# The first batch of a packed-attention and SoLU kernel: Z and the attention weights as two 16-bit parts instead of pairs of 32-bit words

## The chip, the cores and the metric

The kernel runs on one core of a Trainium2 chip. The metric is the time of one execution on the device, in microseconds (us); lower is better. A kernel is timed in several executions, and their median is compared. One more execution is recorded by the profiler; all durations below come from that one.

## What is computed

Eight batches with 8 heads, 576 query and key rows and 64 columns per head, and 32 packed queries `p` per head. Two attentions follow each other, and a layer of 512 to 1024 to 512 columns works on their output:

```python
def sm_attn(qq, kk, vv):
    s = scale * np.matmul(qq, kk.transpose(0, 1, 3, 2))
    s = s - np.max(s, axis=-1, keepdims=True)
    a = np.exp(s)
    a = a / (np.sum(a, axis=-1, keepdims=True) + 1e-09)
    return np.matmul(a, vv)
p_packed = sm_attn(p, k, v)
out = sm_attn(q, p_packed, p_packed)
...
h = x @ w_in
e = np.exp(h - np.max(h, axis=-1, keepdims=True))
sm = e / (np.sum(e, axis=-1, keepdims=True) + 1e-09)
solu = h * sm
...
ln = (solu - mu) / np.sqrt(var + 1e-06) * g_ln
return (ln @ w_out).astype(np.float32)
```

Here `x` is `out` with the heads side by side: 4608 tokens of 512 columns. The weights `w_in` and `w_out` arrive as 64-bit numbers.

## The kernel before

**The work.** For each batch the packed attention gives 32 rows per head (`pack`, flows k0 to k7), transposed in the tile `ppT`. The second attention never forms its output: `make_z` (flows z0 to z7) multiplies the packed rows by `w_in`, so that a batch has a matrix Z of 256 rows and 1024 columns, and `unpack` (q0 to q7) makes the attention weights `a` of 576 query rows on those 256 rows. A token tile of 128 rows (`token_tile`, t0 to t35) is then h = a Z, followed by softmax, product, normalisation, a transpose by DMA, and the product with `w_out`. As 576 is four and a half times 128, every fifth token tile (t4, t13, t22, t31) takes its upper 64 rows from an even batch and its lower 64 from the odd batch behind it; it is called a shared tile below. A shared tile issues 24 matmuls with 64 columns of weights, where a plain tile issues 12 with 128.

**Precision.** A product of 32-bit quality is made from two parts: high times high, high times low, low times high (lines 636 and 637). For batches 1 to 7 the parts are 16-bit (F16): `zh`, `zl`, `a_h`, `a_l`. Z is scaled by a power of two that is found on the chip: `pack` sums the squares of the packed rows and takes half the exponent (`size`, lines 459 to 465), `weight_size` (flow N) does so for `w_in` (`weight`), and `z_scale` (line 341) puts them together. For batch 0 the parts are 32-bit words of a type that TensorE rounds (F32R): `z_r` and `a_r`, without a scale (`plain`, line 100, is 1). That has three consequences. `pack(0)` returns before the squares (line 455). N isn't needed before batch 1. And the first shared tile, t4, is written differently from the others (lines 625 and 640): all of its matmuls of one batch, then those of the other, while the other shared tiles alternate between the two batches from one matmul to the next:

```python
for x, r, t in ((x, r, t) for x in range(2) for r in range(2) for t in range(3)) if not c else ((x, r, t) for r in range(2) for t in range(3) for x in range(2)):
```

**How Z is split.** `split` (line 578) has two ways for the later batches: 'a' copies the product from PSUM with the scale (ACT), casts the copy and subtracts; 'l' casts from PSUM with the scale (ACT, line 606) and subtracts from PSUM (DVE, line 608). Batch 0 goes by lines 587 to 594: copy by ACT (589), cast by ACT (591), subtract by DVE or POOL (593). `ZF_BY` chooses. Its weights are cast by ACT (line 529) and subtracted by DVE (531).

**The order of the work.** Everything stands in the string `ORDER`: each name there advances that flow (a generator) to its next `yield`. Each engine carries out its own instructions strictly in that order; semaphores do the rest. Names that begin with l are loads (`lw` w_in, `lo` w_out, `lk`, `lq`, `lv`, `lp`, `lg`); W and O convert the weights to 32 bits, S and C scale `w_out`, H splits `w_in` into 16-bit halves that batches 2 to 7 use, Z is a warm-up of TensorE. PSUM has three tiles `h` of two banks, one `po`, one `pa`. `LOAD_IN` says in which buffers a raw weight waits: 'h' and 'l' are the buffers of `zh` and `zl`, 'r' is one of `raw`. The halves of H lie in the buffers of `a_r` (line 332), so H waits until t4 has used them.

Of the kernel before, what the change touches and what calls it, by code (L numbers as in the profile page):

```python
# [47 lines left out]
def packed_attention_solu_kernel(ctx: ExitStack, tc: tile.TileContext, q: bass.AP, k: bass.AP, v: bass.AP, p: bass.AP, w_in: bass.AP, w_out: bass.AP, g_ln: bass.AP, out: bass.AP):  # L48
# [719 lines left out]
```

## Time and profile before

| | us |
|---|---|
| median of 3 executions | 396.0 |
| lowest, highest | 393.84, 396.99 |
| the profiled execution | 393.78 |
| its span, from the first to the last instruction | 392.0 |

The profiled execution is 1.8 us longer than its span, and 2.2 us under the median. Engines are PE (TensorE's matmuls), PEld (its weight loads, beside the matmuls), DVE (VectorE), ACT (ScalarE), POOL (GpSimd) and SP (which issues the DMAs). Matmuls are pipelined: the duration of one (0.38 us) is longer than the distance from one start to the next. A float32 matmul can show as two records. L641 is line 641 of the kernel.

### The profile page before, as it was taken

To read this page: it belongs to the slowest core of one execution; us is meant where nothing else is said; L and a number is where in the kernel's file an instruction comes from. 1 tells how busy PE (TensorE), PEld (TensorE's weight loads), DVE (VectorE), ACT (ScalarE), POOL (GpSimd) and SP (SyncE) were. 2 spreads that over 40 slices of the span, in tenths; PEclk is the share of its full clock that TensorE was granted. 3 is DMA by queue.
4 is the path that set the end of the run, shared out by engine and by line. 5 is a ranking of instruction groups with operands and counts; after the bars stand their busy time and mean duration, and the time that the engine had idled before them with its cause. 6 is when DMAs were issued, how large, how long until landed. Compare 5 with 4: busy or idle time off the path is not lost.

```text
span 392.0 us, 8802 instructions
## 1 busy us (share of the span) xinstructions
PE 379.0 (97%) x3370; PEld 198.5 (51%) x3370; DVE 303.8 (78%) x484; ACT 251.0 (64%) x424; POOL 254.3 (65%) x442
## 2 busy tenths in 40 slices
PE   8798989989999999999999999999999999999996
PEld 8566666445444544554445445544454444444445
DVE  2758889998997977898879689995888868468541
ACT  2468788586786868585556956755667476546630
POOL 2476599984566886587373855884458768764630
PEclk9969999999999999999999999999999999999999
DMA  8999896879897796999798977936643533334661
GB/s 285 420 363 352 194 208 120 194 147 177 192 187 139 184 214 123 166 174 209 162 171 176 171 143 209 219 83 139 137 89 82 134 80 84 110 80 107 108 161 54
DMA packets 213866, 66.11 MB, mean 169 GB/s; under 512 B 194744, under 2 KB 207808, under 8 KB 213312
## 3 DMA queue, kind: packets, MB, share of 16 engines
q1 hardware_dynamic: 213824, 65.56, 72.7%
q8 instruction: 26, 0.43, 0.5%
q14 instruction: 16, 0.13, 0.1%
HBM read 37.23 MB, written 9.44 MB: 119 GB/s over the span
## 4 chain that ended last, share of the span: by engine, by line
PE 89%; DVE 5%; ACT 4%; issue 1%; POOL 0%; DVEq 0%; POOLq 0%
PE po L698 41%; PE h L641 23%; PE h L698 5%; PE h L366 3%; PE pa L444 3%; PE h L396 2%; PE h L569 2%; PE h L515 2%; PE po L117 2%; PE h L434 2%; PE h L203 1%; PE po L119 1%; DVE s L480 1%; ACT e L223 1%; DVE nm L644 1%
## 5 line engine op out<-in xcount | busy, mean ns | idle before, releaser
L698 PE MATMUL po<-wch,yT 128*128 128x512 f16 x512 | 160.1, 379 | 1.2 <-ACT o_sb L704 1.2
L698 PEld LDWEIGHTS <-yT 128*128 128x128 f16 x888 | 85.5, 98 | 103.2 <-issue 5.9
L698 PE MATMUL po<-wcl,yT 128*128 128x512 f16 x256 | 97.0, 379 | 0.0
L672 ACT ACTIVATE yhl<-u,negmu 128x1024 f16<-128x1024 f32 x36 | 41.2, 1145 | 24.6 <-POOL negmu L669 24.4
L666 DVE SCALAR_TENSOR_TENSOR u<-e,s_row,h 128x1024 f32<-128x1024 f32 x36 | 45.8, 1271 | 14.5 <-POOL s_row L658 7.7
L674 DVE SCALAR_TENSOR_TENSOR yhl<-u,negmu,yhl 128x1024 f16<-128x1024 f32 x36 | 48.1, 1335 | 6.1 <-ACT yhl L672 5.7
L644 DVE TENSOR_REDUCE nm<-h 128x1 f32<-128x1024 f32 x36 | 43.7, 1213 | 5.5 <-PE h L641 5.3
L641 PE MATMUL h<-zl,a_h 128*128 128x512 f16 (+1 forms) x160 | 47.8, 380 | 0.0
L680 ACT ACTIVATE e<-u,negmu 128x1024 f32<-128x1024 f32 x36 | 41.0, 1139 | 0.0
L662 ACT ACTIVATE e<-h,nmc,z_scale 128x1024 f32<-128x1024 f32 x32 | 38.4, 1198 | 3.7 <-DVE nmc L647 3.0
L641 PEld LDWEIGHTS <-a_h 128*128 128x128 f16 (+1 forms) x280 | 25.1, 101 | 28.1 <-issue 1.4
L649 ACT ACTIVATE nmc<-nm,z_scale 128x1 f32<-128x1 f32 x29 | 8.5, 292 | 45.4 <-DVE nm L644 45.4
L652 POOL TENSOR_SCALAR bound<-nm,z_scale 128x1 f32<-128x1 f32 x31 | 15.5, 500 | 32.1 <-DVE nm L644 30.2
L641 PE MATMUL h<-zh,a_h 128*128 128x512 f16 (+1 forms) x120 | 35.8, 380 | 0.0
L706 DVE TENSOR_SCALAR o_sb<-po,c_row,inv 128x512 f32<-128x512 f32 x24 | 19.3, 806 | 16.1 <-PE po L698 13.6
L641 PE MATMUL h<-zl,a_l 128*128 128x512 f16 (+1 forms) x80 | 30.3, 379 | 0.0
L688 POOL TENSOR_TENSOR c_row<-c_row,neg_half 128x1 f32<-128x1 f32 x36 | 24.5, 681 | 3.0
L669 POOL TENSOR_SCALAR negmu<-su 128x1 f32<-128x1 f32 x36 | 8.8, 244 | 23.2 <-DVE u L666 20.2
L641 PE MATMUL h<-zh,a_l 128*128 128x512 f16 (+1 forms) x60 | 22.7, 379 | 0.0
L486 POOL TENSOR_TENSOR s<-s,mx 128x576 f32<-128x576 f32 x14 | 17.1, 1228 | 8.2 <-DVE mx L484 8.2
L499 POOL TENSOR_TENSOR a<-a,sm 128x576 f32<-128x576 f32 x16 | 19.7, 1238 | 3.7 <-DVE sm L497 3.1
L531 POOL TENSOR_TENSOR a_l<-s,a_h 128x576 f16<-128x576 f32 x14 | 18.4, 1320 | 4.6 <-ACT a_h L529 4.6
(184 smaller groups left out, 727.7 us busy)
## 6 DMA issues: line engine op xcount, KB each, us to landing
out_dram<-o_sb SPq DMA_DIRECT2D x35, 256.0 KB, 2.3
v_sb<-in_v_dram SPq DMA_DIRECT2D x8, 1024.0 KB, 6.7
raw<-in_k_dram SPq DMA_DIRECT2D x24, 288.0 KB, 4.7
raw<-in_q_dram SPq DMA_DIRECT2D x96, 72.0 KB, 2.5
zl<-in_moe_w_in_dram SPq DMA_DIRECT2D x2, 1024.0 KB, 7.3
raw<-in_k_dram SPq DMA_DIRECT2D x2, 1024.0 KB, 12.1
raw<-in_moe_w_out_dram SPq DMA_DIRECT2D x2, 1024.0 KB, 9.3
zh<-in_moe_w_in_dram SPq DMA_DIRECT2D x2, 1024.0 KB, 13.9
```

The costliest lines, as they stand in the source:

```text
L499: EN(nc, SOFT_BY[2 * b + 1]).tensor_tensor(out=w2, in0=w2, in1=sm.unsqueeze(2).broadcast_to([P, NB, J]), op=ALU.mult)
L531: EN(nc, A2L_BY[2 * b + r]).tensor_tensor(out=lo, in0=a2T, in1=hi if b else hi.bitcast(F32), op=ALU.subtract)
L641: nc.tensor.matmul(dst_[:, cols], lhsT=lhsT, rhs=z[:, r, cols], start=bool(first), stop=bool(last))
L644: nc.vector.tensor_reduce(out=nm, in_=h, axis=AX.X, op=ALU.max, negate=True)
L662: nc.scalar.activation(e, h, AF.Exp, bias=nmc, scale=sc[:, 1:], accum_out=se)
L666: nc.vector.scalar_tensor_tensor(out=u, in0=e, scalar=s_row, in1=h, op0=ALU.mult, op1=ALU.mult, accum_out=su)
L672: nc.scalar.activation(yhl[:, 0], u, AF.Identity, bias=negmu)
L674: nc.vector.scalar_tensor_tensor(out=yhl[:, 1], in0=u, scalar=negmu, in1=yhl[:, 0], op0=ALU.add, op1=ALU.subtract)
L680: nc.scalar.activation(e, u, AF.Square, bias=negmu, accum_out=sq)
L688: nc.gpsimd.tensor_tensor(out=c_row, in0=c_row, in1=neg_half, op=ALU.pow)
L698: nc.tensor.matmul(po[:, cols], lhsT=yT[:, a, c], rhs=w[:, c, cols], start=c == 0 and t == 0, stop=c == NFC - 1 and t == 2)
L706: nc.vector.tensor_scalar(out=o_sb[:, cols], in0=po[:, cols], scalar1=c_row, scalar2=inv, op0=ALU.mult, op1=ALU.mult)
```

## The change

Batch 0 is treated as batches 1 to 7 are. Its special cases go, its scale is made on the chip, t4 is written as the other shared tiles are, H gets buffers of its own, `ZF_BY` sets batch 0 to 'l', one weight load moves from a `zh` to a `zl` buffer, and `ORDER` is another string. The cut diff:

```diff
-ZF_BY = 'aaaallllaaaaaaaaaaaaaaaaaaaaaaaa'
+ZF_BY = 'llllllllaaaaaaaaaaaaaaaaaaaaaaaa'
...
-LOAD_IN = 'hlhlrhrh'
+LOAD_IN = 'hlhlrhrl'
...
-ORDER = 'lw1 lp W1 W1 lk0 W1 Z W1 lo0 lw3 O0 lw2 k0 k0 lp O0 O0 W3
+ORDER = 'lw2 Z W2 lk0 W2 lo0 lp O0 W2 k0 O0 p p k0 lw3 k0 O0 W2 lw1
...
-    a_r = [par.tile([P, 2, S], F32R, name='a_r', bufs=2) for i in range(2)]
...
-        hi = [par.tile([P, 4 * S], F16, name='a_r', bufs=2)[:, :2 * DF].rearrange('p (g f) -> p g f', g=2) for _ in range(2)]
+        hi = [par.tile([P, 2 * DF], F16, name='w_hi', bufs=2).rearrange('p (g f) -> p g f', g=2) for _ in range(2)]
...
-        if not b:
-            return
         squares = att.tile([P, 2 * D], F32, name='squares')
...
-            hi, lo = (a_h[b % 2][:, r], a_l[b % 2][:, r]) if b else (a_r[0][:, r], a_r[1][:, r])
+            hi, lo = (a_h[b % 2][:, r], a_l[b % 2][:, r])
...
-                elif not b:
-                    full = whole[0][:, r, cols]
-                    nc.scalar.copy(full, pz)
-                    yield
-                    copy_by(nc, ZH_BY[at])(z_r[0][:, r, cols], full)
-                    yield
-                    EN(nc, ZL_BY[at]).tensor_tensor(out=z_r[1][:, r, cols], in0=full, in1=z_r[0].bitcast(F32)[:, r, cols], op=ALU.subtract)
-                    yield
...
-            for x, r, t in ((x, r, t) for x in range(2) for r in range(2) for t in range(3)) if not c else ((x, r, t) for r in range(2) for t in range(3) for x in range(2)):
+            for r, t, x in ((r, t, x) for r in range(2) for t in range(3) for x in range(2)):
                 left = slice(0, LEFT) if x else slice(MAIN, S)
-                a_hi, a_lo, z_hi, z_lo = (a_h[x], a_l[x], zh[c + x], zl[c + x]) if c + x else (a_r[0], a_r[1], z_r[0], z_r[1])
+                a_hi, a_lo, z_hi, z_lo = (a_h[x], a_l[x], zh[c + x], zl[c + x])
...
-            for dst_, lhsT, z, r, first, last in terms[6:] + terms[:6] if b is None and not c and n else terms:
+            for dst_, lhsT, z, r, first, last in terms:
                 nc.tensor.matmul(dst_[:, cols], lhsT=lhsT, rhs=z[:, r, cols], start=bool(first), stop=bool(last))
```

**Three places in the order of the instructions.** On PE, where batch 0's second attention and its Z begin (`ppT` is batch 0's; L506 are the scores, L575 the products of Z, L271 a column sum for a scale), before:

```order
L450 MATMUL pa<-ident,pp 128x128
L180 MATMUL po<-ident,g_raw 128x8
L506 MATMUL h<-qT,ppT 32x288 x4
L203 MATMUL h<-ident,e 64x128 x8
L506 MATMUL h<-qT,ppT 32x288 x12
L575 MATMUL h<-w_in_sb,ppT 32x512 x8
L271 MATMUL pa<-ssq,ones_f 128x8
```

The same place now (L500 are the scores, L564 the products, L455 the sum of batch 0's squares, L267 a column sum):

```order
L446 MATMUL pa<-ident,pp 128x128
L368 MATMUL h<-ident,raw 128x128 x2
L199 MATMUL h<-ident,e 64x128 x8
L455 MATMUL pa<-total,ones_f 128x1
L500 MATMUL h<-qT,ppT 32x288 x4
L176 MATMUL po<-ident,g_raw 128x8
L267 MATMUL pa<-wsq,ones_f 128x4
L500 MATMUL h<-qT,ppT 32x288 x8
L564 MATMUL h<-w_in_sb,ppT 32x512 x4
L500 MATMUL h<-qT,ppT 32x288 x4
L564 MATMUL h<-w_in_sb,ppT 32x512 x4
```

The two sums that batch 0's scale needs, of the squares and of `wsq` (the size of `w_in`), have moved between and ahead of the first scores; the sum of `wsq` stood far behind, after t3.

On DVE, the same stretch, from the copy that makes `ppT` on (`s_443` and `s_444` are the scores of the even and the odd heads), before:

```order
L453 COPY ppT<-pa 128x128
L244 TENSOR_REDUCE ssq<-raw 128x2
L480 STREAM_TRANSPOSE s_443<-h 128x288
L225 TENSOR_SCALAR yT<-e 128x1024
L480 STREAM_TRANSPOSE s_443<-h 128x288
L480 STREAM_TRANSPOSE s_444<-h 128x288
L244 TENSOR_REDUCE ssq<-zh 128x2
```

And now:

```order
L449 COPY ppT<-pa 128x128
L240 TENSOR_REDUCE ssq<-raw 128x2
L310 TENSOR_SCALAR size<-pa 128x1
L311 TENSOR_SCALAR size<-size 128x1
L245 TENSOR_SCALAR wsq<-wsq 128x4
L246 TENSOR_SCALAR wsq<-wsq 128x4
L316 SCALAR_TENSOR_TENSOR wsq<-wsq 128x4
L474 STREAM_TRANSPOSE s_452<-h 128x288
L269 TENSOR_REDUCE w_size<-pa 128x1
L310 TENSOR_SCALAR w_size<-w_size 128x1
L311 TENSOR_SCALAR w_size<-w_size 128x1
L319 TENSOR_SCALAR w_size<-w_size 128x1
```

Nine small instructions (two for `size`, three for `wsq`, four for `w_size`) now stand around the first transpose of scores, and two more, for `z_scale`, follow behind them.

On PE, the first shared tile, t4 (batch 0 has the first number of `zh` and `zl`, batch 1 the second), before:

```order
L641 MATMUL h_1180<-zh_495,a_r_117 64x512
L641 MATMUL h_1180<-zl_496,a_r_117 64x512
L641 MATMUL h_1180<-zh_495,a_r_118 64x512
L641 LDWEIGHTS a_h1_120
L641 MATMUL h_1180<-zl_1003,a_h1_120 64x512
```

And now:

```order
L617 LDWEIGHTS a_h0_114
L617 MATMUL h_1225<-zh_498,a_h0_114 64x512
L617 LDWEIGHTS a_h1_115
L617 MATMUL h_1225<-zl_1022,a_h1_115 64x512
L617 LDWEIGHTS a_h0_114
L617 MATMUL h_1225<-zh_498,a_h0_114 64x512
L617 LDWEIGHTS a_h1_115
L617 MATMUL h_1225<-zl_1022,a_h1_115 64x512
```

Batch 0's matmuls stood together, ahead of batch 1's; now they alternate from the first on. Ahead of t4 the order before has 54 of the matmuls with `w_out` (L698), the new one has 72 (L674).

## Rows read from the trace of the kernel before

**Rows 1.** The page, part 1: busy us, share of the span, instructions, by engine.

```profile
PE 379.0 (97%) x3370; PEld 198.5 (51%) x3370; DVE 303.8 (78%) x484; ACT 251.0 (64%) x424; POOL 254.3 (65%) x442
```

**Rows 2.** Windows: stretch, length, busy us (instructions) by engine, granted clock, DMA share, GB/s.

```profile
20.00:30.00 10.00, 9.66 (x92) 6.88 (x94) 5.58 (x8) 5.75 (x10) 7.57 (x4) 0.66 1.10 357
30.00:54.00 24.00, 20.80 (x379) 14.38 (x376) 20.53 (x38) 20.45 (x33) 15.76 (x10) 1.00 0.99 270
54.00:95.00 41.00, 38.95 (x329) 21.64 (x329) 37.74 (x70) 30.49 (x55) 33.77 (x52) 1.00 0.81 155
95.00:389.00 294.00, 293.81 (x2431) 141.31 (x2430) 230.09 (x361) 186.90 (x321) 189.33 (x359) 1.00 0.68 145
```

**Rows 3.** Waits of PE: who waited for whom, us in total, times, longest.

```profile
PE h L396 <- ACT pT L209: 3.5, 1, 3.5
...
PE po L698 <- ACT o_sb L704: 1.2, 1, 1.2
...
PE pa L271 <- DVE ssq L280: 0.7, 1, 0.7
```

**Rows 4.** Timeline of PE: start, us, engine, line, operation, tiles, count.

```profile
55.11 0.62 PE L641 MATMUL h<-zh,a_r 128*128 128x512 f32 x2
55.57 0.39 PE L641 MATMUL h<-zl,a_r 128*128 128x512 f32 x1
55.80 0.61 PE L641 MATMUL h<-zh,a_r 128*128 128x512 f32 x2
...
66.70 0.38 PE L461 MATMUL pa<-total,ones_f 128*128 128x1 f32 x2
66.94 0.48 PE L641 MATMUL h<-zh,a_r 128*128 128x512 f32 x1
```

**Rows 5.** The chain that ended last: start, us, what; w_out's 24 matmuls, three shared tiles.

```profile
161.55 5.18 PE po L698 x24
...
89.48 5.70 PE h L641 x24
...
178.49 2.78 PE h L641 x24
...
261.02 2.71 PE h L641 x24
```

**Rows 6.** Windows of DVE alone: stretch, length, busy us (instructions), clock, DMA share, GB/s.

```profile
35.45:56.30 20.85, 18.33 (x35) 1.00 1.02 229
...
80.00:120.00 40.00, 36.81 (x63) 1.00 0.85 171
```

**Rows 7.** Timeline of DVE: batch 0's subtractions, then the small instructions of batch 1's scale.

```profile
42.87 2.28 DVE L593 TENSOR_TENSOR zl<-zf,zh 128x512 fp32r<-128x512 f32 x2
...
49.84 1.36 DVE L531 TENSOR_TENSOR a_r<-s,a_r 128x576 fp32r<-128x576 f32 x1 [0.42 <-ACT a_r L529]
...
53.84 0.88 DVE L531 TENSOR_TENSOR a_r<-s,a_r 128x576 fp32r<-128x576 f32 x1 [0.64 <-ACT a_r L529]
54.64 1.65 DVE L593 TENSOR_TENSOR zl<-zf,zh 128x512 fp32r<-128x512 f32 x1
...
68.93 0.15 DVE L315 TENSOR_SCALAR size<-size 128x1 int32<-128x1 int32 x1
...
69.42 1.09 DVE L320 SCALAR_TENSOR_TENSOR wsq<-wsq 128x4 f32<-128x4 f32 x1
...
72.90 0.41 DVE L344 TENSOR_TENSOR z_scale<-w_size,size 128x1 int32<-128x1 int32 x1
...
183.79 0.75 DVE L486 TENSOR_TENSOR s<-s,mx 128x576 f32<-128x576 f32 x1
```

**Rows 8.** Batch 1's subtraction of Z: count, ns min/median/max, first and last start, forms.

```profile
L608 DVE SCALAR_TENSOR_TENSOR zl<-h,z_scale,zl x4: 654/710/751, 83.5 to 92.3; 128x512 f16<-128x512 f32 x4
```

**Rows 9.** Timeline of PE: the same kind of matmul within, and behind, the slow stretch.

```profile
21.47 1.84 PE L203 MATMUL h<-ident,e 128*64 128x128 f32 x16
23.24 2.16 PE L396 MATMUL h<-kT,pT 64*32 64x288 f32 x16
25.34 3.48 PE L366 MATMUL h<-ident,raw 128*64 128x128 f32 x32
...
29.77 1.09 PE L203 MATMUL h<-ident,e 128*64 128x128 f32 x16
...
31.16 1.97 PE L366 MATMUL h<-ident,raw 128*64 128x128 f32 x32
```

More of the change, by code (lines that the diff above doesn't have):

```diff
@@ L99, in packed_attention_solu_kernel @@
     nc.gpsimd.memset(neg_one, -1.0)
-    plain = const.tile([P, 2], F32, name='plain')
-    nc.gpsimd.memset(plain[:, :1], 1.0)
-    nc.gpsimd.memset(plain[:, 1:], 1.0 / A_MAX)
     e1 = const.tile([P, 2, S + LEFT], F32, name='e1')
@@ L527, in unpack @@
             yield
-            hi, lo = (a_h[b % 2][:, r], a_l[b % 2][:, r]) if b else (a_r[0][:, r], a_r[1][:, r])
+            hi, lo = (a_h[b % 2][:, r], a_l[b % 2][:, r])
             nc.scalar.copy(hi, a2T)
             yield
-            EN(nc, A2L_BY[2 * b + r]).tensor_tensor(out=lo, in0=a2T, in1=hi if b else hi.bitcast(F32), op=ALU.subtract)
+            EN(nc, A2L_BY[2 * b + r]).tensor_tensor(out=lo, in0=a2T, in1=hi, op=ALU.subtract)
             yield
@@ L535, in make_z @@
         ppT = packed[b]
-        if b:
-            z_scale(b)
-            s_z = zsc[b][:, :1]
-            if b % 2:
-                sc = zsc[b - 1, b] = small.tile([P, 2], F32, name='z_scale2')
-                for x in range(2):
-                    nc.gpsimd.tensor_copy(sc[LEFT * x:LEFT * x + LEFT], zsc.get(b - 1 + x, plain)[LEFT * x:LEFT * x + LEFT])
-            yield
-            parts = par.tile([P, 2, 2, DF], F16, name='zl' if b % 2 else 'zh', bufs=2)
-            zh[b], zl[b] = (parts[:, 0], parts[:, 1])
-            if ZP_BY[b] == '1':
-                s_z = 1.0 / A_MAX
-                s_p = small.tile([P, 1], F32, name='s_p')
-                nc.vector.tensor_scalar(out=s_p.bitcast(I32), in0=size[b].bitcast(I32), scalar1=-1, scalar2=188 << 23, op0=ALU.mult, op1=ALU.add)
-                pph = att.tile([P, 2, P], F16, name='pph')
-                nc.scalar.activation(pph[:, 0], ppT, AF.Copy, scale=s_p)
-                yield
-                nc.vector.scalar_tensor_tensor(out=pph[:, 1], in0=ppT, scalar=s_p, in1=pph[:, 0], op0=ALU.mult, op1=ALU.subtract)
-                yield
-        else:
-            z_r.extend(par.tile([P, 2 * DF], F32R, name=name, bufs=2).rearrange('p (r f) -> p r f', r=2) for name in ('zh', 'zl'))
-            if ZF_BY[0] == 'a':
-                whole[0] = par.tile([P, 2, DF], F32, name='zf')
+        z_scale(b)
+        s_z = zsc[b][:, :1]
+        if b % 2:
+            sc = zsc[b - 1, b] = small.tile([P, 2], F32, name='z_scale2')
+            for x in range(2):
+                nc.gpsimd.tensor_copy(sc[LEFT * x:LEFT * x + LEFT], zsc[b - 1 + x][LEFT * x:LEFT * x + LEFT])
+        yield
+        parts = par.tile([P, 2, 2, DF], F16, name='zl' if b % 2 else 'zh', bufs=2)
+        zh[b], zl[b] = (parts[:, 0], parts[:, 1])
+        if ZP_BY[b] == '1':
+            s_z = 1.0 / A_MAX
+            s_p = small.tile([P, 1], F32, name='s_p')
+            nc.vector.tensor_scalar(out=s_p.bitcast(I32), in0=size[b].bitcast(I32), scalar1=-1, scalar2=188 << 23, op0=ALU.mult, op1=ALU.add)
+            pph = att.tile([P, 2, P], F16, name='pph')
+            nc.scalar.activation(pph[:, 0], ppT, AF.Copy, scale=s_p)
+            yield
+            nc.vector.scalar_tensor_tensor(out=pph[:, 1], in0=ppT, scalar=s_p, in1=pph[:, 0], op0=ALU.mult, op1=ALU.subtract)
+            yield
         banks = [[], []]
@@ L581, in split @@
                 at = 4 * b + 2 * n + r
-                if not b and ZF_BY[0] == 'l':
-                    nc.scalar.copy(z_r[0][:, r, cols], pz)
-                    yield
-                    nc.vector.tensor_tensor(out=z_r[1][:, r, cols], in0=pz, in1=z_r[0].bitcast(F32)[:, r, cols], op=ALU.subtract)
-                    yield
-                elif not b:
-                    full = whole[0][:, r, cols]
-                    nc.scalar.copy(full, pz)
-                    yield
-                    copy_by(nc, ZH_BY[at])(z_r[0][:, r, cols], full)
-                    yield
-                    EN(nc, ZL_BY[at]).tensor_tensor(out=z_r[1][:, r, cols], in0=full, in1=z_r[0].bitcast(F32)[:, r, cols], op=ALU.subtract)
-                    yield
-                elif ZF_BY[at] == 'a':
+                if ZF_BY[at] == 'a':
                     if b not in whole:
```

8 lines of the change are left out of this document (4 added, 4 removed).

## The prediction

> **What bounds the kernel now.** I read the shares of the engines first. PE is busy for 379.0 of 392.0 us, DVE 304, ACT and POOL some 250 [rows 1]. The table by stretches says where the other 13 us lie: from 95 to 389 us PE is busy for 293.81 of 294 us, from 54 to 95 for 38.95 of 41, and only before 54 does it miss more [rows 2]. So from 54 us on the reader is to see a queue of matmuls without holes. Whatever shortens that queue ends the kernel earlier by as much, as long as the other engines follow; whatever delays its beginning is paid in full. The waits of PE name the holes ahead of it: one of 3.5 us for the transposed `p`, smaller ones of 1.2 and 0.7 us [rows 3]. The last view is the chain that ended last, which gives the length of the pieces of the queue [rows 5].
>
> **The change part by part.** The profiled execution took 393.78 us, 1.8 more than its span; I make the sum against it and carry it over to the median of 396.0.
>
> *The 16-bit form.* t0 to t3 have 48 matmuls on words of 32 bits. Three of them take 55.80 - 55.11 = 0.69 us from start to start, 0.230 each [rows 4]. The 16-bit matmuls with `w_out`, of the same 512 columns, take 5.18 us for 24, 0.216 each [rows 5]. 48 x 0.014 = 0.7 us less. Nothing hides this: the matmuls lie in the queue.
> [...]
>
> *The first shared tile.* t4's 24 matmuls take 5.70 us, those of the next two shared tiles 2.78 and 2.71 [rows 5]. All have 64 columns of weights; the later ones alternate between the upper and the lower 64 rows of `h`, and two of them run in the time of one. t4 will be written as they are: 5.70 - 2.74 = 2.96 us less. The bound on the other side is a new wait. Before, t4 began with batch 0's parts alone; now its second half needs batch 1's Z by its first matmul. Batch 1's last subtraction starts at 92.3 and takes 0.75 us [rows 8], so the last part is there at 93.0, while t4 began at 89.48 [rows 5]. At these times t4's first 12 matmuls would be done at 89.48 + 1.37 = 90.85 and the others would wait 2.2 us: 0.8 us would be left of the gain. But the new order puts 72 matmuls with `w_out` ahead of t4 instead of 54; 18 x 0.216 = 3.9 us, which is more than the wait. I take no wait and keep 2.2 us for the range.
>
> *One more column sum.* Batch 0's squares need a matmul pair of 66.94 - 66.70 = 0.24 us [rows 4]. The sum over `wsq` is only moved. Plus 0.2.
>
> *The start of t0.* Here DVE decides: it is busy for 18.33 of 20.85 us between `ppT` and t0's last operand [rows 6]. Up to the second subtraction of the weights, which ends at 53.84 + 0.88 = 54.72, I remove two subtractions of Z (2.28 together) and two of weights (1.36 and 0.88): 4.5 us [rows 7]. I add four subtractions from PSUM of 0.71 each [rows 8], 2.8 us, the weights' subtractions to 16 bits, and eleven small instructions. For the weights the trace has no row in this place on DVE; a DVE subtraction of the same size takes 0.75, and what is removed up to 1.36, so 1.5 to 2.7 for the two, of which I take 1.5, the row that nothing disturbed. The small ones take 0.15 each, but one took 1.09 and one 0.41 [rows 7]: 1.65 to 2.85 together. That is 5.9 to 8.3 us added, and net 1.4 to 3.8. The 2.5 us in which DVE had nothing to do in this stretch can take in part of it. I take 0.8 us later, 55.5. But then all of Z is there already, while before its last part came only at 54.64 + 1.65 = 56.29 [rows 7]. t0 and the first half of t1 are 18 matmuls. Before, at least eight of them stood behind that last part: 56.29 + 8 x 0.230 = 58.1. Now 13 stand behind the second subtraction of the weights: 55.5 + 13 x 0.216 = 58.3. The term is zero; its bounds are 0.6 less (all of it taken in) and 3.2 more (nothing taken in, 58.5 + 2.8 = 61.3).
>
> *What costs nothing.* ACT loses four casts of Z and POOL one subtraction; neither is near its limit [rows 1]. H no longer waits for t4's buffers; it feeds batch 2's Z, which PE reaches in the full stretch. The loads are the same bytes but in another order, `k0` and the first weights still lead, and the first scores wait for `p` and `k0` as before. The middle and the end have the same matmuls in another sequence. Its cover is PE's own queue, and in 95 to 389 it can get worse by what DVE can't follow: DVE is busy for 36.81 of 40 us from 80 to 120 [rows 6], the least slack of any engine.
>
> Sum: -0.7 - 2.96 + 0.24 + 0 = -3.4 us; 390.4 for the profiled execution, **392.6** for the median, 0.9% faster. About 1% is what a measurement of this kernel can tell from no change. With the bounds of the single terms the forecast's own range is 391 to 395.
>
> **The rivals.**
>
> *More than the queue (390.8).* From 54 to 95 us PE stood still for 41.0 - 38.95 = 2.05 us [rows 2], 1.2 of them for the bank `po`, which ACT had not emptied [rows 3]. The small instructions of N and the scale of batch 1, among them the one of 1.09 us, stood in DVE's queue at 69 to 73 us [rows 7] ahead of what the first token tiles need, and most of them now stand earlier. The new order also has four products of Z and eight scores between t0's and t1's matmuls with `w_out`, and twelve more products of Z behind. If these holes close, 1.8 us more go: -5.2. Against it: another order usually opens other holes.
>
> *Given back at the hand-overs (395.5).* The matmuls are shorter as worked out, but t0 starts late or t4 waits for batch 1's Z. Either bound alone (3.2 or 2.2 us) leaves -0.2 to -1.2; I put it at -0.5. For it: the sum over `wsq` stands on PE ahead of the second scores and waits for DVE's fifth small instruction, and all scores and products of Z wait behind it on PE. Against it: in the same place PE waited for DVE before too.
>
> *Slower: a slow stretch of the clock between 36 and 45 us (399).* Behind the wait of 3.5 us for `p` the granted clock was 0.66 on the mean of 20 to 30 us [rows 2, 3], which mixes 1.2 and 2.4 GHz. The same eight matmuls took 1.84 us there and 1.09 behind it, the transposes 3.48 and 1.97 [rows 9]. With about 1.1 for the scores' 2.16 that is 0.8 + 1.1 + 1.5 = 3.3 us for one slow stretch. The mechanism: after `ppT`, PE has one quarter of the scores and then the sum over `wsq`. If that holds it for as long as `p` did, the clock falls again, and PE loses 3.5 us standing and 3.3 slow: -3.4 + 6.8 = +3.4 us. It decides only if DVE brings `wsq` over 3 us late; below, the clock stays as in 30 to 54, where PE missed 3.2 us in pieces and had 1.00 [rows 2]. DVE's queue up to there is one reduction and five small instructions, some 2.5 us, less the scores: it comes near, but should not get there.
>
> *The change doesn't do what it says.* If t4's pairs didn't run side by side, only 0.7 us would be left, less 0.24. Three other shared tiles with the same code speak against it; I count it with the second rival.
>
> **How the numbers follow.** Forecast 0.50, more than the queue 0.24, given back 0.17, slow stretch 0.09. Over 1% faster is below 392.0: nearly all of the first rival (0.22) and two fifths of the forecast, whose bound is only 0.6 us away (0.20): 0.42. Slower by over 1% is above 400: the upper part of the slow stretch and a new order whose holes in the middle add up: 0.07. The rest, 0.51, lies within 1%. The range goes from 388.5, somewhat below the first rival, to 396.5, just above the second.
>
> **What would show it.** Right: t4's 24 matmuls in 2.7 to 2.8 us; three matmuls of t0 to t3 in 0.65; PE still full from 95 us on; the first matmul of t0 between 53 and 55 us; the last matmul at about 385.4 of the span. Wrong: a wait of PE over 2 us for `wsq` or for the weights' subtraction, a granted clock below 1 between 36 and 54 us, a wait ahead of t4's second matmul, or more than 2 us of idle PE from 95 to the end.

## The result: 0.6% slower, and the profile after

The changed kernel takes 397.59 us (median of 11 runs, 396.34 to 400.97), the kernel before, run beside it, 395.72. The ratio is 1.006, with a 95% interval of 1.0032 to 1.0089. Forecast were 392.6, in a range of 388.5 to 396.5: the time went the other way, and out of the range by 1.1 us.

The profiled execution took 397.08 us. That of before, 393.78, is among the quickest of its kernel (18 of its 107 timed executions had the same mean granted clock, 0.991, and took 393.5 to 394.9 us; the others had 0.982 to 0.987 and took 394.9 to 397.5), so the two spans lie 3.3 us apart where the medians lie 1.9 apart, and some 1.4 us of what the two traces show as difference is between executions.

Part 1 of the page after, as [rows 1]:

```profile
PE 377.7 (96%) x3372; PEld 195.7 (50%) x3372; DVE 302.7 (77%) x489; ACT 249.7 (63%) x422; POOL 253.5 (64%) x439
```

The table by stretches, as [rows 2]:

```profile
20.00:30.00 10.00, 7.18 (x77) 5.80 (x78) 7.27 (x9) 5.44 (x9) 6.41 (x4) 0.50 1.09 345
30.00:54.00 24.00, 21.28 (x347) 14.32 (x343) 18.16 (x47) 16.70 (x27) 13.33 (x9) 1.00 1.14 246
54.00:95.00 41.00, 37.74 (x366) 18.92 (x367) 37.80 (x65) 33.35 (x57) 34.05 (x50) 1.00 0.99 169
95.00:389.00 294.00, 291.75 (x2417) 139.27 (x2416) 230.94 (x362) 186.89 (x324) 191.12 (x361) 1.00 0.78 145
```

PE has 1.3 us less work in all, but it now stands still for 3.26 us from 54 to 95 (2.05 before) and for 2.25 from 95 to 389 (0.19 before). The queue of matmuls, which was closed, has holes. The waits of PE name them, as [rows 3]; the first two, and that for `inv`, lie ahead of 54 us:

```profile
PE h L392 <- ACT kT L370: 2.5, 1, 2.5
PE h L362 <- DMA raw<-in_q_dram: 2.2, 1, 2.2
PE po L674 <- DMA yT<-yhl: 1.9, 3, 0.9
...
PE h L362 <- DVE inv L269: 1.0, 1, 1.0
PE pa L440 <- ACT e1T L432: 1.0, 1, 1.0
...
PE h L362 <- DVE zh L584: 0.8, 1, 0.8
PE h L674 <- DVE o_sb L682: 0.7, 1, 0.7
PE h L617 <- POOL a_l L525: 0.6, 1, 0.6
```

PE's timeline shows the beginning of the queue and t4; a first column of 57.54 is the start of t0:

```profile
47.41 1.97 PE L362 MATMUL h<-ident,raw 128*64 128x128 f32 x32 [1.04 <-DVE inv L269]
...
52.57 1.19 PE L392 MATMUL h<-kT,pT 64*32 64x288 f32 x16
54.52 1.97 PE L362 MATMUL h<-ident,raw 128*64 128x128 f32 x32 [0.76 <-DVE zh L584]
56.41 1.19 PE L392 MATMUL h<-kT,pT 64*32 64x288 f32 x16
57.54 0.60 PE L617 MATMUL h<-zh,a_h 128*128 128x512 f16 x2
...
58.20 0.59 PE L617 MATMUL h<-zh,a_h 128*128 128x512 f16 x2
...
95.91 0.40 PE L617 MATMUL h<-zh,a_h 128*64 128x512 f16 x1
95.91 0.40 PE L617 MATMUL h<-zl,a_h 128*64 128x512 f16 x1
...
98.29 0.40 PE L617 MATMUL h<-zl,a_l 128*64 128x512 f16 x1 [0.58 <-POOL a_l L525]
```

t0 starts at 57.54, 3.7 us later than before (53.85). Of these, 1.2 arise ahead of `ppT`, which is copied at 36.37 instead of 35.16, and 2.5 behind it. From t0 to the last matmul it is 334.6 us, as before (335.0): the 3.4 us that the sum promised have shrunk to 0.4. So there are two questions: what holds t0, and who ate the rest.

For the first, the windows from the copy of `ppT` to t0's first matmul, before and then now, say how much of the 2.5 us is work of PE (the first pair of numbers) and how much is waiting:

```profile
35.16:53.85 18.69, 15.54 (x246) 10.08 (x246) 16.17 (x33) 16.04 (x28) 12.48 (x9) 1.00 0.98 237
36.37:57.54 21.17, 18.35 (x251) 11.34 (x250) 16.72 (x44) 15.24 (x26) 11.17 (x8) 1.00 1.16 224
```

PE is busy for 2.8 us more with nearly the same matmuls, and idle for 2.8 us where it was idle for 3.15.

A first look at the waiting is ACT's timeline of batch 0's Z (the bracket is the idle time ahead, and whom ACT waited for):

```profile
43.23 0.69 ACT L582 ACTIVATE zh<-h,z_scale 128x512 f16<-128x512 f32 x1 [1.72 <-PE h L564]
45.80 0.69 ACT L582 ACTIVATE zh<-h,z_scale 128x512 f16<-128x512 f32 x1 [1.88 <-DVE zh L584]
46.38 1.00 ACT L364 COPY kT<-h 128x1024 f32<-128x1024 f32 x1
...
52.99 0.69 ACT L582 ACTIVATE zh<-h,z_scale 128x512 f16<-128x512 f32 x1 [0.91 <-DVE zh L584]
```

The second cast of each pair waits until DVE has made the first subtraction, though it needs nothing of it; both read the same tile `h`, each its own bank of it. (Another reason would be that the cast writes the tile `zh` that the subtraction reads. Against it, the second cast of a pair ran at 43.50 in the kernel before, within the first subtraction of 42.87 to 44.5.) The second subtraction then comes late too, and PE's transposes of q and k need the tile that it frees. It runs until 47.27, `inv` is the small instruction of DVE right behind it, and the transposes start at 47.41 (the row of PE above):

```profile
46.52 0.75 DVE L584 SCALAR_TENSOR_TENSOR zh<-h,z_scale,zh 128x512 f16<-128x512 f32 x1 [0.75 <-ACT zh L582]
```

This is the **hand-over theory**. Its rival is the **order theory**: the new sequence costs, whatever the form of Z.

### The profile page after: what moved, and what is told of

Read it like the earlier page. It is cut to its first block, busy times and chain, and to the rows that moved or that the text cites. A ratio compares the mean times of both kernels' runs of the same rounds, so it can differ in the third digit from the quotient of the medians.

```text
span 395.3 us, 8802 instructions
## 1 busy us (share of the span) xinstructions
PE 377.7 (96%) x3372; PEld 195.7 (50%) x3372; DVE 302.7 (77%) x489; ACT 249.7 (63%) x422; POOL 253.5 (64%) x439
## 4 chain that ended last, share of the span: by engine, by line
PE 72%; DMA 8%; POOL 6%; SPq 4%; ACT 4%; DVE 4%; issue 1%; DVEq 0%; POOLq 0%
PE po L674 36%; PE h L617 20%; PE h L674 5%; DMA raw<-in_q_dram 5%; SPq L149 3%; POOL wcl L303 2%; PE h L558 2%; DMA raw<-in_k_dram 2%; PE h L362 2%; PE pa L440 2%; PE h L430 1%; SPq L653 1%; DMA yT<-yhl 1%; PE h L509 1%; PE h L392 1%
## 5 line engine op out<-in xcount | busy, mean ns | idle before, releaser
L674 PE MATMUL po<-wch,yT 128*128 128x512 f16 x512 | 160.7, 379 | 1.9 <-DMA yT<-yhl 1.9
L674 PEld LDWEIGHTS <-yT 128*128 128x128 f16 x888 | 85.6, 98 | 102.7 <-DMA yT<-yhl 4.7
L674 PE MATMUL po<-wcl,yT 128*128 128x512 f16 x256 | 97.0, 379 | 0.0
L650 DVE SCALAR_TENSOR_TENSOR yhl<-u,negmu,yhl 128x1024 f16<-128x1024 f32 x36 | 49.4, 1373 | 6.5 <-ACT yhl L648 6.1
L638 ACT ACTIVATE e<-h,nmc,z_scale 128x1024 f32<-128x1024 f32 x36 | 43.3, 1202 | 8.5 <-DVE nmc L623 7.6
L617 PE MATMUL h<-zh,a_h 128*128 128x512 f16 (+1 forms) x160 | 47.8, 380 | 0.1
L617 PEld LDWEIGHTS <-a_h 128*128 128x128 f16 (+1 forms) x320 | 28.1, 101 | 33.4 <-issue 2.2
L628 POOL TENSOR_SCALAR bound<-nm,z_scale 128x1 f32<-128x1 f32 x33 | 18.3, 555 | 36.2 <-DVE nm L620 34.7
L617 PE MATMUL h<-zh,a_l 128*128 128x512 f16 (+1 forms) x80 | 30.3, 379 | 0.0
L664 POOL TENSOR_TENSOR c_row<-c_row,neg_half 128x1 f32<-128x1 f32 x36 | 22.7, 632 | 3.0
L617 PEld LDWEIGHTS <-a_l 128*128 128x128 f16 (+1 forms) x160 | 14.6, 100 | 18.8 <-POOL a_l L525 1.7
L634 POOL TENSOR_TENSOR s_row<-bound,neg_one 128x1 f32<-128x1 f32 x33 | 20.2, 613 | 2.7
L362 PE MATMUL h<-ident,raw 128*64 128x128 f32 x256 | 17.4, 294 | 4.0 <-DMA raw<-in_q_dram 2.2
```

The source lines that it names most:

```text
L362: nc.tensor.matmul(pt[64 * r:64 * r + 64, g * MAIN + c * P:g * MAIN + (c + 1) * P], lhsT=rows[:, c, 2 * (g0 + g) + r], rhs=ident, start=Tr ...
L617: nc.tensor.matmul(dst_[:, cols], lhsT=lhsT, rhs=z[:, r, cols], start=bool(first), stop=bool(last))
L634: nc.gpsimd.tensor_tensor(out=s_row, in0=bound, in1=neg_one, op=ALU.pow)
L638: nc.scalar.activation(e, h, AF.Exp, bias=nmc, scale=sc[:, 1:], accum_out=se)
L650: nc.vector.scalar_tensor_tensor(out=yhl[:, 1], in0=u, scalar=negmu, in1=yhl[:, 0], op0=ALU.add, op1=ALU.subtract)
L664: nc.gpsimd.tensor_tensor(out=c_row, in0=c_row, in1=neg_half, op=ALU.pow)
```

## The experiments

**Form and order apart.** `a_old_order` is the changed code with the sequence of the kernel before, fitted to its steps; `a_old_order_n` has the weights' size early in it; `b_new_order` is the code of before in the new sequence, with H moved behind t4. `c_t4_apart` is the changed kernel with t4's matmuls written as before:

```diff
-            for r, t, x in ((r, t, x) for r in range(2) for t in range(3) for x in range(2)):
+            for x, r, t in ((x, r, t) for x in range(2) for r in range(2) for t in range(3)) if not c else (...):
```

> The changed code under the order of before; only what the change needs is put in (the sum of the squares, the sum over wsq behind ppT, the scale ahead of Z; one cast fewer per part of Z). Theory 'order': the new order string is what costs, in its head and in the holes up to 110 us, and the code is worth the 3.4 us that were forecast. Then t0's first matmul starts at 53.9 plus or minus 0.7 us, and the time is 1.5 to 3.5 us under before (ratio 0.991 to 0.996). Theory 'form': the scale and the hand-over of Z between ACT and DVE through PSUM make t0 late under any order. Then t0 starts at 56 us or later, and the time is that of before or above it (ratio 0.999 to 1.004).

> As a_old_order, but the sum over wsq stands some 12 us earlier, between the two exponentials of k0, where DVE has little to do; so only the squares and the scale itself are left behind ppT. If the chain that makes the scale is what delays t0 ('form'), t0 starts 0.5 to 1.5 us earlier than in a_old_order and the time falls by as much; by 'order' the two agree within 0.5 us.

> The code of before (pairs of 32-bit words, no scale for batch 0) under the new order; H behind t4, as its buffers need. 'order': the lateness stays without the gain, t0 starts after 56 us, and the time is 2 to 5 us above before (ratio 1.005 to 1.013). 'form': t0 starts at 54 to 55 us and the time is within 1 us of before.

> The changed kernel, but t4's matmuls stand as before, those of batch 0 first, and don't alternate. If the pairs are worth what the rows of the later shared tiles say, t4's 24 matmuls take 5.2 to 5.7 us and the time rises by 2.3 to 3 us against the changed kernel (ratio to before about 1.012). If t4 only waits for batch 1's Z and weights instead, it starts with batch 0's parts while these are made, and the time rises by 1.3 us or less.

Medians and ratios to before: 404.88 us, 1.0237 [1.0194, 1.0281]; 403.11, 1.0187 [1.0145, 1.023]; 399.87, 1.0107 [1.0063, 1.0152]; 398.17, 1.0057 [1.0036, 1.0078]. Neither theory alone: each form is slow in the other's sequence. In the new sequence the 16-bit code is the better one (397.6 against 399.9), in the old one it loses 7 to 9 us.

For t0 alone `b_new_order` is clear. `ppT` is copied at 34.40 and t0 starts at 55.50, 21.1 us later, as in the changed kernel (21.2) and not as before (18.7), and here too PE has more work, not more waiting:

```profile
34.40:55.50 21.10, 18.09 (x249) 11.04 (x247) 17.32 (x39) 17.17 (x28) 13.67 (x9) 1.00 1.09 248
```

So the new sequence alone makes PE's work ahead of t0 2.6 us longer, without any 16-bit word. (The time of this run says less: behind t4, where H now stands, PE is busy for 15.03 of 18 us from 95 to 113.)

In the old sequence the hand-over is longest, though `ppT` itself is copied only at 38.65 in `a_old_order`, which the hand-over doesn't explain. ACT's casts there:

```profile
49.55 0.69 ACT L582 ACTIVATE zh<-h,z_scale 128x512 f16<-128x512 f32 x1 [2.77 <-DVE zh L584]
...
57.02 0.69 ACT L582 ACTIVATE zh<-h,z_scale 128x512 f16<-128x512 f32 x1 [1.78 <-DVE zh L584]
```

and PE, behind them, waits for the copy `qT` and then runs at a slow clock (as many of the same matmuls took 1.19 us at 56.32; the granted clock is 0.92 on the mean of 54 to 95):

```profile
60.33 2.17 PE L392 MATMUL h<-kT,pT 64*32 64x288 f32 x16 [2.81 <-ACT qT L364]
```

`c_t4_apart`: t4 un-paired takes 6.1 us (95.07 to 101.2) instead of 4.4, but the median is only 0.6 us worse and the intervals overlap. Something behind t4 absorbs most of what t4 gains.

**The hand-over alone.** `d2_casts_first` keeps the changed kernel's sequence, but in batch 0's Z both casts of a pair stand ahead of both subtractions. `a2_old_casts_first` does it in `a_old_order_n`. `d3_by_copy` goes through the 32-bit copy instead, and `d2_tail` adds six matmuls of t34 between t35's halves.

```diff
-            for r, pz in enumerate(banks[n]):
-                (cast r; subtraction r)
+            for r, pz in enumerate(banks[n]):
+                (cast r)
+            for r, pz in enumerate(banks[n]):
+                (subtraction r)
```

> The changed kernel, its order of instructions kept, but in batch 0's Z both casts of a pair of banks stand ahead of both subtractions, so that ScalarE's second cast no longer waits for VectorE's first subtraction. Hand-over theory (that wait is what makes t0 late behind ppT): the two waits of 1.88 and 0.91 us at ScalarE go, ppT stays at 36.4 and t0 starts at 55.2 to 56.5 instead of 57.54; the run gets 1 to 2.3 us faster than the changed kernel, 395 to 396.6 by the median. Rival (the waits lie in cover, t0 waits for the attention weights' parts, which hang on the head alone): t0 within 0.4 us of 57.54 and the time within 0.5 us of 397.6.

> The changed code in the order of the kernel before, the weights' size early, and both casts of batch 0's Z ahead of both subtractions. Hand-over theory: the waits of about 2.8 and 1.8 us at ScalarE for the first subtraction go, TensorE's wait of 2.8 us for qT behind them goes with the second stretch of slow clock that followed it; t0 starts 3 to 6 us earlier and the time falls from 403.1 to 397 to 400. Rival (the order is what costs: this code's loads and head don't fit it): 402 to 403.5, the waits move to another place.

> The changed kernel, but batch 0's Z goes through a 32-bit copy, as in the kernel before: ScalarE copies with the scale, casts from the copy, VectorE or GpSimd subtract from it. Hand-over theory: TensorE's banks come free after one copy, ScalarE never waits for VectorE inside Z; it does four copies of about 0.7 us more, so t0 starts at 55.5 to 57 and the run is 0.5 to 2 us faster than the changed kernel. Rival (ScalarE's extra work is worth as much as the wait): t0 at 57.5 to 58.5 and the time 397.5 to 398.5.

> As the run with the casts first, and in the tail six w_out matmuls of t34 stand between the two halves of t35's, as in the kernel before. Theory (the second half waits for the first one's copy out of PSUM): the wait of 0.70 us ahead of t35's second half goes, the span ends 0.7 to 0.9 us earlier than with the casts first alone. Rival (t34's last copy is then late and its store ends the span): within 0.3 us of that run.

`d2_casts_first`: 396.3 us, 1.0028 [1.001, 1.0046]. The waits of ACT are gone, `ppT` stays (36.30), and t0 starts 1.26 us earlier:

```profile
43.16 1.26 ACT L571 ACTIVATE zh<-h,z_scale 128x512 f16<-128x512 f32 x2 [1.72 <-PE h L564]
45.03 1.01 ACT L364 COPY kT<-h 128x1024 f32<-128x1024 f32 x1 [0.61 <-PE h L362]
```

```profile
55.15 1.19 PE L392 MATMUL h<-kT,pT 64*32 64x288 f32 x16
56.28 0.61 PE L625 MATMUL h<-zh,a_h 128*128 128x512 f16 x2
```

PE's work from `ppT` to t0 is the same 18.35 us as in the changed kernel; only its idle time has become 1.2 us shorter. The medians differ by as much (1.3 us), but their intervals overlap a little, so it is the trace that shows it.

```profile
36.30:56.28 19.98, 18.35 (x252) 11.35 (x250) 16.86 (x45) 15.68 (x26) 11.71 (x8) 1.00 1.09 217
```

`a2_old_casts_first`: 400.71 against 403.11 us, t0 at 61.34 instead of 64.20, the wait for `qT` 1.2 instead of 2.8. The hand-over theory holds in both sequences, at 1.3 and 2.4 us; in the old one part of the gain is the clock, as the second 16 scores take 1.29 us instead of 2.17 behind the shorter wait.

`d3_by_copy`: 398.51 us, 1.0084 [1.0059, 1.0109]; t0 at 59.89. A miss, and the trace doesn't say what the copies cost: this execution waited 4.3 us for q, and the granted clock from 36 to 54 us was 0.81. `d2_tail`: 396.55 us, 1.0032 [1.0003, 1.0061], no difference. The wait of 0.69 went, and one of 0.45 for `yT` took its place.

**The same form in the kernel before.** `e4_before_l` changes one table of the kernel before; batch 0's Z stays in 32-bit words, but is cast and subtracted straight from PSUM.

```diff
-ZF_BY = 'aaaallllaaaaaaaaaaaaaaaaaaaaaaaa'
+ZF_BY = 'llllllllaaaaaaaaaaaaaaaaaaaaaaaa'
```

> The kernel before in its own order with one table changed: batch 0's Z in 32-bit words is cast straight from PSUM and subtracted from PSUM, without the 32-bit copy, as the changed kernel does with 16-bit words. Hand-over theory: ScalarE's second cast waits for VectorE's first subtraction here too; the copies of q and k behind it come later, TensorE waits longer than 1.3 us for qT, t0 starts 1 to 4 us later than 53.85 and the time is 396.5 to 400 instead of 395.6, without any 16-bit word. Rival (four copies fewer on ScalarE and the subtractions off GpSimd are worth more): 394 to 396, t0 at 53 to 54.

397.33 us, 1.0042 [1.0014, 1.0071]: 1.7 us slower than before without any 16-bit word. From the copy of `ppT` (36.57) to t0 (56.55) it is 20.0 us instead of 18.7, and PE's waits for ACT's copies have grown from the 1.3 for `qT` of before, while its work has not (14.97 us):

```profile
PE h L366 <- ACT qT L368: 2.2, 1, 2.2
...
PE h L366 <- ACT kT L368: 0.7, 1, 0.7
```

The size is as expected, but the cause is not shown to be the hand-over. ACT's second cast waits 0.83 us for the first subtraction, at one pair of the two. Its longer waits in this stretch are others: 1.31 for POOL's `s` and 1.41 for DVE's `s`, whose queue now holds all four subtractions of Z. And as this form has one step fewer for each part, the same `ORDER` brings the later products of Z to PE earlier.

**Who eats t4's gain: operands, loads, the head.** `e1_t4_parts` puts the casts first for batch 1 too (`if b < 2`) and makes batch 1's `a_l` on DVE (`A2L_BY` 'ddpp' to 'dddd'). `e2_transposes` also issues twelve transposes to `yT` on SP ahead of the loads that stood right in front of them, t0's ahead of three. `e3_q_first` also exchanges the tokens `lw0` and `lq0`.

> The run with batch 0's casts first, and the same for batch 1's Z, whose attention weights' low parts are made by VectorE instead of GpSimd. Theory (t4's 24 matmuls lost their gain in waiting for batch 1's parts: 4.9 us from 93.80 to 98.7 instead of 24/2 x 0.22 = 2.6): the two waits for GpSimd's a_l (0.73 and 0.59 us) and the one for zl (0.23) go, t4 takes 2.7 to 3.3 us, the time falls by 1.2 to 2 us to 394.3 to 395.1. Rival (the parts are late from batch 1's scores on, so another operand is waited for in their place): t4 above 4.2 us and the time within 0.5 us of 396.3.

> As the run before in this list, and on SyncE's queue twelve tiles' transposes to yT issued ahead of the loads of later batches that stood right in front of them. Theory (TensorE's waits for yT, 1.2 us at 225 and up to 0.9 in t0 to t3, come from loads queued ahead): these waits go, 0.8 to 1.5 us faster than the run before. Rival (the loads are late in their place, and TensorE waits for raw): within 0.4 us or slower.

> As the run before in this list, and in the head batch 0's q is loaded ahead of the last of the four w_in loads, the two changed over. Theory (the head's 1.1 to 1.2 us come from q landing after 24 us): TensorE's wait of 2.2 to 4.3 us for raw<-q falls under 1, ppT is copied at 33.5 to 35.5 instead of 36.3, t0 starts about 1 us earlier, and the time falls by 0.8 to 1.5 us. Rival (the last part of w_in is then late, and the weights' size and Z wait for it): ppT earlier but t0 not, or a wait for wsq above 1 us; time within 0.5 us or slower.

`e1_t4_parts`: 396.82 us, 1.0036 [1.0013, 1.0059], no gain. The waits for `a_l` are gone, and 21 of t4's matmuls run in 2.4 us, but then one wait stands where three were:

```profile
99.81 0.38 PE L625 MATMUL h<-zl,a_h 128*64 128x512 f16 x1 [1.50 <-DVE zl L574]
```

`e2_transposes`: 421.4 us, 1.0658 [1.0622, 1.0694]. SP works its queue in order: t0's transpose, for which SP has to wait until 66.78, now stands ahead of loads of k and q that went out from 54.21 and 62.00 on in `d2_casts_first`, and batch 1's and later batches' inputs come late. Between 60 and 80 us 107 GB/s are moved instead of 172 there (152 in `e1_t4_parts`). PE waits 6.0 us ahead of 86.7, and further on 4.1, 3.7 and 2.5 us at 143, 241 and 272; the mean granted clock is 0.967 instead of 0.987. No run moved t0's transpose by itself, so its share of the 25 us is not known.

```profile
PE po L682 <- DMA yT<-yhl: 6.0, 1, 6.0
```

`e3_q_first`: 426.46 us, 1.0784 [1.0743, 1.0825]. The wait for q is gone, but ACT stands behind the late part of `w_in`; PE waits 4.5 us for it and t0 starts at 61.01 instead of 56.19. The rival held in both.

**t4 behind other work.** `f1_t4_later` takes `d2_casts_first` and moves t4's two steps behind six matmuls of t3 and the product with v:

```diff
-... z1 t4 H t4 k2 t3 k2 t2 t3 H t4 t3 ...
+... z1 H t3 t3 t3 k2 k2 t2 H t4 t4 t4 ...
```

`f2_waits` also exchanges two pairs of neighbours (t16's transpose with one load of q; t1's copy `o_sb` with t2's squares), `f3_tail` adds the tail of `d2_tail`.

> The run with batch 0's casts first, and t4's 24 matmuls moved behind the 6 w_out matmuls of t3 and the product with v that stood right behind them (2.6 us of work that needs nothing of batch 1's Z). Theory (t4's alternating matmuls take 2.7 us, and what they lost is waiting for batch 1's parts, which are made by 98.5): t4 starts at about 96.4 and takes 2.7 to 3.1 us instead of 4.9, no wait for a_l or zl above 0.3 us is left, and the time falls by 1.2 to 1.8 us against 396.3. Rival (the wait moves on: t4's nm, its Exp or the product with v is late in its place): a new wait of 1 us or more between 93 and 110, time within 0.5 us of 396.3.

> As the run before in this list, with two pairs of neighbours changed over: t16's transpose to yT ahead of the one load of four pieces of q that stood in front of it on SyncE, and t1's copy out of PSUM ahead of t2's squares on ScalarE. Theory (a single late transpose and a late copy cost 1.2 us each; the loss of 25 us came from loads stuck behind t0's transpose): the waits for yT at 225 and for o_sb at 88.5 go, 1.5 to 2.4 us faster than the run before, near 392.5 to 393.5. Rival (any transpose ahead of a load starves a later batch; or t0's to t3's chain is late as a whole and the next wait takes the place): slower, or within 0.5 us.

> As the run before in this list, and the tail with six matmuls of t34 between t35's halves. Theory (wait of 0.70 replaced by 0.45 for yT in the tail, as the run with the tail showed): 0.2 to 0.5 us faster. Rival: no difference within 0.3 us.

401.08 us, 1.0127 [1.0089, 1.0165]; 400.81, 1.0121 [1.0089, 1.0154]; 402.03, 1.0153 [1.0103, 1.0203]. In `f1_t4_later` t4's 24 matmuls took 2.9 us (101.14 to 104.04) without a wait inside, so the matmuls' price is as forecast. But the move had put PE behind two others, and behind the first the granted clock was 0.86 from 93 to 100:

```profile
97.07 0.38 PE L682 MATMUL po<-wch,yT 128*128 128x512 f16 x1 [3.34 <-ACT o_sb L688]
...
105.68 0.30 PE L446 MATMUL pa<-ident,pp 128*128 128x128 f32 x1 [1.64 <-DVE pp L443]
```

`f2_waits` lost one of the two waits for `o_sb`, as meant, and gained no time; `f3_tail` cannot be told from it.

`g1_t4_between` moves what released these two as well: t2's `o_sb` ahead on ACT, the scaling `pp` ahead of t4's maximum on DVE. `g2_both` adds the two pairs of neighbours.

```diff
-... t2 t2 q1 z1 q1 z1 t2 t2 ... z1 t4 H t4 k2 t3 k2 t2 t3 H t4 t3 lq3 k2 ...
+... t2 t2 t2 t2 q1 z1 q1 z1 ... z1 H k2 k2 t3 t2 t3 t3 t4 t4 k2 H t4 lq3 ...
```

> The run with batch 0's casts first, and t4 behind the product with v and six w_out matmuls of t3 as in the run that moved it before, but without the two waits that this move had made: t2's copy out of PSUM stands ahead of batch 1's last attention weights on ScalarE (it freed the bank 3.3 us late), and the scaling of batch 1's product ahead of t4's maximum on VectorE (1.6 us). Theory (t4's matmuls keep their gain once their operands are ready and nothing new waits): from the last w_out matmul of t2 at 93.7 to the transposition of batch 1's product 6.1 us instead of 7.9, no wait above 0.9 us between 93 and 107, 1.5 to 2 us faster than 396.3. Rival (these parts are so tight that each move opens another wait of the same size): within 0.5 us of 396.3 or slower.

> As the run before in this list, with the two pairs of neighbours changed over (t16's transpose ahead of one load of q, t1's copy out of PSUM ahead of t2's squares), which took two waits away in the run with the waits. Theory: 1 to 2 us faster than the run before in this list, near 393. Rival: the lateness moves on, within 0.5 us.

396.33 us, 1.0018 [1.0001, 1.0036], against 396.3 for `d2_casts_first`, and 397.18, 1.005 [1.0018, 1.0083] for `g2_both`: neither gained what was expected. In `g1_t4_between` t4 takes 2.8 us, and the transposition behind it starts at 99.71 instead of 101.64. Eight us later the 1.9 us are gone. PE, then the stretch by engine:

```profile
105.52 0.72 PE L509 MATMUL h<-qT,ppT 64*32 64x288 f32 x16 [0.85 <-DVE qT L375]
...
108.58 0.60 PE L625 MATMUL h<-zl,a_h 128*128 128x512 f16 x2 [0.49 <-DVE size L310]
```

```profile
95.00:113.00 18.00, 16.65 (x169) 7.47 (x166) 17.34 (x30) 12.05 (x21) 11.96 (x22) 1.00 0.84 140
```

The 1.9 us went into these two waits and into the scores that the first of them cuts in two: with the wait they take 2.6 us from 103.97 on, where `d2_casts_first` has 1.13 for the 32 in one piece. Both waits end with DVE, which (third pair of numbers) is busy for 17.34 of 18 us. A full DVE alone doesn't stop PE, as before it was busy for 17.55 of the same 18 us with PE at 18.00. So the next run asks whether it does here.

**DVE's order.** `h1_vector` is `g1_t4_between` with three instructions of DVE moved forward: two subtractions of `w_in`'s low half, one of them into a wait of 1.49 us for batch 1's Z, and one transposition of `qT`.

```diff
-... q1 z1 q1 z1 ... z1 H k2 k2 ... t4 t4 k2 H t4 lq3 H k2 ... t5 t4 t4 q2 ...
+... q1 H z1 q1 z1 ... z1 k2 k2 ... t4 t4 k2 H H t4 lq3 k2 ... t5 q2 t4 t4 ...
```

> The run with t4 in between, and only VectorE's order changed at three places of 93 to 105: a subtraction of the weights' low half goes into VectorE's wait of 1.49 us for batch 1's Z, another ahead of t4's maximum, and a transposition of batch 2's q ahead of t4's scaled product. Theory (from 95 to 113 VectorE, busy 17.3 of 18 us, sets the pace, so TensorE's 1.9 us came back as waits of 0.85 for qT and 0.49 for the size): VectorE is 1.2 us ahead at t4's maximum, those two waits shrink by 0.8 to 1.3 us together, t5's first matmul behind them (108.58) starts 0.8 to 1.3 us earlier, and the time falls from 396.3 to 395.0 to 395.6. Rival (another engine's chain, such as SyncE's loads or ScalarE, holds these parts): the two waits stay within 0.3 us, or move to raw, and the time stays within 0.4 us of 396.3.

395.89 us, 1.0008 [0.9984, 1.0032]. The wait for `qT` is gone, that for the size has grown to 1.30, and t5's first matmul behind it starts 0.83 us earlier:

```profile
107.75 0.60 PE L625 MATMUL h<-zl,a_h 128*128 128x512 f16 x2 [1.30 <-DVE size L310]
```

The span is 0.9 us shorter than that of `g1_t4_between` (393.3 and 394.2), the median 0.4. Of the 0.83 us, 0.13 was there ahead of the moved instructions. The trace bears the theory out in part: DVE's order moved t5 by what was expected, at the low end, but the two waits didn't shrink (1.30 us together, 1.34 in `g1_t4_between`). What became shorter is the 32 scores, 1.2 us in one piece again. The intervals of the two times overlap, so the time doesn't show it. This version of the changed code has the lowest median: it takes back the loss, and cannot be told from the kernel before. None of the runs is faster than the kernel before.

## Why the prediction was wrong, step by step

**The 16-bit form: right.** Three matmuls of t0 take 58.20 - 57.54 = 0.66 us, and 0.65 further on, as forecast; -0.7 us is in.

**The start of t0: the step that failed.** "Here DVE decides", and the term was put at zero: I added up DVE's durations, took PE's own work as longer by one column sum of 0.2 us, and let four subtractions from PSUM stand as independent work. Behind `ppT` t0 came 2.5 us later. DVE was not busy for much longer than before (16.72 us as against 16.17). PE was, by 2.8 us (18.35 and 15.54), and `b_new_order` has 2.6 of these with the old form of Z: it is the sequence. Against that, PE's waits became 0.3 us shorter in all, and they would have become 1.5 us shorter without the hand-over, which is worth 1.2 us, as `d2_casts_first` shows: DVE's second subtraction frees the tile late, not for its own time but for the cast that it waits for. So t0 would have come 1.3 us late even with the casts first. The small instructions, which I feared at up to 2.85 us, were cheap: 0.13 to 0.17 each, the scale ready at 40.8.

Where PE's 2.8 us lie I read from rows; no run changed one of these places by itself. Two column sums, one new and that of `wsq` from further behind, and two transposes that had stood ahead of `ppT` are busy for some 1.2 us. The rest is matmuls that have lost their neighbours: the 32 products of batch 0's Z are busy for 3.5 us before and 4.2 now, the 32 scores of batch 1 for 1.25 and 2.38. The first half of these scores is 16 matmuls on rows 0 to 63 of PE's array, the second 16 on rows 64 to 127. In the old sequence they stand next to each other and run side by side:

```profile
49.40 1.25 PE L396 MATMUL h<-kT,pT 64*32 64x288 f32 x32
```

In the new one 32 transposes stand between them, and they take 1.19 us twice (`b_new_order`: 1.20 twice). That is 2.38 - 1.25 = 1.13 us more. It was to be seen in the order of the instructions; I compared what stands there, not which neighbours run together. The Trainium skill, page "TensorE: Matmul & The Clock Gate", section "Part 3: Packing small matmuls — row/col tiling", says that matmuls on different row and column groups of the array run at the same time; the trace agrees, with 1.25 us for 32 and 1.19 for 16.

**The first shared tile: the matmuls right, the term wrong.** With its operands there, t4 took 2.8 to 2.9 us, forecast 2.74. In the changed kernel it took 4.4, because it waited for `a_l` and `zl` of batch 1. The parts `a_l` of its attention weights I had not looked at; the wait for Z I had excluded by holding the end of batch 1's last subtraction (93.0 in the trace before) against 72 matmuls of new cover. But a time from the old trace is no date: in the new sequence that subtraction ended at 99.7. And even without the wait the gain was gone 8 us later, in waits that end with DVE, which `h1_vector` bears out in part. From t0 to the last matmul it is 334.9 us in `d2_casts_first`, 334.6 in `g1_t4_between` and 334.1 in `h1_vector`: no run with t4 in 2.8 us has taken the forecast 3.4 us off the 335.0 of before. [rows 6] had a warning, DVE busy for 36.81 of 40 us from 80 to 120; I named it as "the least slack of any engine" and still booked PE's 2.96 us in full.

**One more column sum:** +0.24 forecast, about 0.3 measured (37.50 to 37.81). Right; it lies ahead of t0 and is part of the 2.8.

**What costs nothing: wrong, in small pieces.** Up to three waits for `yT` (1.9 us together), one in the tail (0.7), one for `e1T` (1.0); "its cover is PE's own queue" held as long as the old sequence kept it closed. Behind t0 the 16-bit form and t4 gave 0.7 and 1.3 us, and the stretch became 0.4 shorter; the other 1.6 us, by an estimate from these rows, are in such waits. The moves tried in f and g mended none of it: each opened waits of about its own size or more. The 1.2 us ahead of `ppT` I don't put down to the change. In `e4_before_l` PE's and SP's sequence up to there is that of before, and yet `ppT` was copied at 36.57 instead of 35.16. The stretch 20 to 30 us has a granted clock of 0.52 there and 0.66 in [rows 2]; the changed kernel's profile has 0.50 and 36.37.

**The rivals.** "Given back at the hand-overs" came nearest, at 395.5 with a chance of 0.17. Its outcome was the right one, a late t0 and a t4 that waits; I had let only one of its two bounds come true, and most of both did (2.5 of 3.2 us, and 1.7 of 2.2). Its reason was not: PE waited for `wsq` by 0.1 us or less, and at t4 for `a_l` before it waited for Z. The range of 391 to 395 doesn't follow from the terms either: one bound at a time they give 392.0 to 395.8, and both upper ones together 398.0, above the 397.6 measured.

The slow stretch of clock did not come in the changed kernel's profile (1.00 from 36 us on). But it did in `a_old_order`, behind a wait of 2.8 us and not of "over 3 us"; and in `f3_tail` the granted clock was 0.72 from 36 to 54, in an execution in which PE had waited 4.1 us for q until 25.1 and in that stretch itself never over 0.8; its t0 started at 60.68, its mean clock was 0.978. Of the changed kernel's own eleven executions three had a mean clock of 0.979 and took 399.38 to 400.97 us, about the 399 of this rival; the other eight had 0.983 to 0.991 and stayed under 398.4. None of the three was profiled, so that they lost it in the same place is not shown.

Of the four signs of a wrong forecast one appeared as put, 2.25 us of idle PE from 95 on. A second nearly did: t4 waited, but ahead of its sixth and twelfth matmuls, not its second. The wait for `wsq` and the slow clock did not. Of the five signs of a right one four failed: t0's start, t4's 2.7 us, a full PE from 95 on and the end of the span. The 0.65 us for three matmuls came true.

What stays open: the split scores and products were not put together again in the new sequence, so their price stands on rows and on `b_new_order`; whether the program or the chip makes the second cast wait is not shown; and which of the loads or ACT's copies sets the head was not settled.

## What to carry to other kernels

Look at which matmuls are neighbours, not only at which stand in the queue: taken apart, the same ones can take longer. Casts and subtractions that read one PSUM tile were a chain over two engines here: put all casts first, and look for what needs the tile. A gain on the busiest engine can be lost where its next instruction waits for a second engine that is full; read the windows of exactly that stretch, before and again after each move. And a time taken from the old trace may not serve as a due date in a new sequence: follow the chain that makes the operand.

## What the hardware showed beyond that

Matmuls that use different parts of PE's array ran side by side when they were neighbours, for 32-bit and 16-bit words alike: 32 scores in 1.25 us where 16 take 1.19, and 24 matmuls of 64 columns in 2.8 us where un-paired ones took 5.7. Twelve transposes put ahead of loads in SP's queue cost 25 us; the first of them, which waited until 66.78, held three loads. And the head, which has the same instructions, took 1.4 us more in one execution than in another, with the granted clock at 0.52 and 0.66: a term below that can't be read from a single pair of profiles.
